# Moving the first pair of w_in ahead of x, and both even products of Q in front of its odd ones

## The chip, the cores and the metric

The kernel runs on one core of a Trainium2 chip. The metric is the device time of one execution in microseconds (us). The profile's span is 1.7 to 3.0 us shorter than the time of the same run, 1.8 in most. The granted clock is the share of TensorE's full clock that the profile records: 1.00 is full, 0.50 half. PE is TensorE, DVE is VectorE, ACT is ScalarE, POOL is GpSimd; SPq and ACTq are the queues from which the sync and the scalar engine issue transfers.

## The reference

```python
# x: (8, 3008, 256), float32; w_in: (256, 2048), w_out: (2048, 256), float64; result float32
X = np.fft.fft(np.fft.fft(x, axis=1), axis=2).real      # mixing
h = X.reshape(8 * 3008, 256) @ w_in
return (np.maximum(h, 0) ** 2 @ w_out)                  # squared ReLU between two products
```

## The kernel before

The transform over the sequence is done by products with cosine and sine tables (cosT, sinT) of folded x; that gives Pt, Qt and Et. The transform over the 256 columns is folded into w_in: G is w_in multiplied by small tables (cosd, sind, altd). The weights come as float64, and each pair of column blocks of w_in ("pair j", eight in all) is first rounded to float32, partly on VectorE, partly on ScalarE. `load_win(j)` issues the transfer and the first part of the rounding; what it returns finishes it and multiplies:

```python
def convert(dst, src):
    ...                                        # raw <- transfer of the pair's 64-bit words
    nc.vector.tensor_scalar(out=eb, in0=high, ...)              # fd<-raw
    act(e, eb, AF.Relu, ...); act(eb, e, AF.Relu, ...)          # fd<-fd, ScalarE
    nc.vector.tensor_scalar(out=mb, in0=high, ...)              # fs<-raw
    act(rest, low, AF.Copy, scale=2.0 ** -32)                   # raw<-raw, ScalarE
    def finish():
        nc.vector.scalar_tensor_tensor(out=eb, ...)             # fd<-raw,fd
        tt(out=m, in0=mb, in1=rest, op=ALU.add)                 # fs<-fs,raw
        nc.vector.scalar_tensor_tensor(out=dst, ...)            # win<-fs,fd
    return finish

def load_win(j):
    w = ep.tile(...)
    finish = convert(w, pair_in(j))
    def then():
        finish()
        for tab, G, n in ((cosd, G1, P), (sind, G2, P - 1)):
            ps = psh.tile([P, CH], F32, name="pg", tag="h")
            ... # pg: 2 products each, copied to G by ScalarE
        ps = psd.tile([P, CH], F32, name="pe", tag="d")
        ...     # pe: 4 products of one column, copied to gE
    return then
```

A transform (`group`) has an even product, two joins on VectorE, and an odd product; the even and odd results lie in tiles of PSUM (the memory that the products here are written to), named "pd", of a pool with two buffers (`psd`), which the pe tiles share. Then comes the main loop over the 8 batches; its first eight steps still round and multiply pairs 2 to 7 and the blocks of w_out.

The first phase of the kernel before, in order of issue (cut):

```python
for t in range(NT):                    # NT = 7 tiles of x
    load_x(0, t)
load_table(cosT, cos_s, nc.sync)
load_table(sinT, sin_s, nc.sync)
for dst, src in ((cosd, cos_d), (sind, sin_d), (altd, alt_d)):
    nc.sync.dma_start(out=dst, in_=...)
...                                    # fold x, make Pt and Et, fold for Q
begun = weights.pop(0)()               # pair 0: transfer, first part of rounding
for f in groups[16:20]:                # Q, rows of even number: even product, joins, odd product
    f()
next_weight()                          # begin pair 1; finish and multiply pair 0
for f in groups[20:]:                  # Q, the other half
    f()
next_weight()                          # begin pair 2; finish and multiply pair 1
```

## Time and profile before

| | before |
|---|---|
| median of the first three runs | 2075.13 us (2070.41 to 2075.86) |
| span of the profiled run | 2067.1 us |
| TensorE busy | 2004.5 us, 97% of the span |
| TensorE not busy | 62.6 us: 41.6 before 122 us, 10.5 in the last 51.7 us |
| median over all 35 timed runs of this study | between 2070.06 and 2072.77 us by set of runs (2067.44 to 2075.86) |

What is not TensorE's work is 62.6 us, 3% of the span, so what a new order of the first phase can take from TensorE's waiting is a few per cent at most. Time at half clock counts as busy here (from 62.24 to 71.80 us TensorE is busy for 9.55 of 9.56 us, at a granted clock of 0.54); the experiments come back to it. The views that carry this, windows and chain of waits, stand in the prediction.

### The profile page before, as it was taken

Reading aid. Unit: us, or ns where it says so; the run is one execution under the profiler, and the core shown is the slowest. Engines: PE = TensorE matmul, PEld = TensorE weight load, DVE = VectorE, ACT = ScalarE, POOL = GpSimd, SP = SyncE. Lnnn points to the kernel's source line nnn. Section 1 sums busy time; section 2 is a strip of 40 time slices with the busy share of each in tenths; the row PEclk is TensorE's granted clock in tenths of the full one; section 3 lists DMA queues with packets and bytes.
Section 4 is the critical chain, followed back from the end, with each engine's and each line's share of the span. In section 5 each row is a group of like instructions: output and inputs, shape, how many; then the busy total and the mean of one; then the engine's idle time right before and its main releaser. Section 6 shows DMA issues by size and latency. Waiting matters only on the chain.

```text
span 2067.1 us, 27083 instructions
## 1 busy us (share of the span) xinstructions
PE 2004.5 (97%) x9464; PEld 1742.9 (84%) x9464; DVE 1334.7 (65%) x3271; ACT 949.4 (46%) x1069; POOL 1202.6 (58%) x1766
## 2 busy tenths in 40 slices
PE   5799999999999999999999999999999999999997
PEld 3688888888888888888888888888888888888887
DVE  6798665776567755677557775577656775555553
ACT  1554444444444543455444544454444444445443
POOL 0376555665566654666556665566655675456565
PEclk9899999999999999999999999999999999999999
DMA  5333000110011010011001100011001100000000
GB/s 168 91 62 59 29 11 31 41 35 21 11 40 41 26 31 26 26 31 46 11 26 36 38 28 11 31 41 36 21 11 40 41 11 21 26 11 11 21 11 20
DMA packets 66104, 68.45 MB, mean 33 GB/s; under 512 B 26297, under 2 KB 56969, under 8 KB 65968
## 3 DMA queue, kind: packets, MB, share of 16 engines
q1 hardware_dynamic: 65968, 66.73, 11.4%
q8 instruction: 74, 1.21, 0.3%
q14 instruction: 62, 0.51, 0.1%
HBM read 42.03 MB, written 24.68 MB: 32 GB/s over the span
## 4 chain that ended last, share of the span: by engine, by line
PE 94%; DVE 3%; DMA 1%; ACT 0%; issue 0%; SPq 0%; POOL 0%; POOLq 0%; ACTq 0%; DVEq 0%
PE ph L410 16%; PE mA L450 16%; PE ph L411 16%; PE mC L450 16%; PE mB L450 15%; PE mD L450 8%; PE pd L350 5%; PE po L484 2%; PE pg L234 1%; DMA xt<-in_x_dram 1%; ACT os L486 0%; DVE he L413 0%; PE pe L240 0%; DVE g L416 0%; DVE g L415 0%
## 5 line engine op out<-in xcount | busy, mean ns | idle before, releaser
L424 ACT ACTIVATE g<-g 128x1004 f32<-128x1004 f32 (+1 forms) x384 | 399.4, 1040 | 828.0 <-DVE g L416 551.9
L413 DVE SCALAR_TENSOR_TENSOR he<-Et,gE,ph 128x251 f32<-128x251 f32 (+1 forms) x768 | 362.2, 472 | 591.9 <-PE ph L411 591.2
L430 POOL TENSOR_TENSOR s<-g 128x251 f32<-128x251 f32 (+1 forms) x384 | 251.7, 655 | 686.3 <-ACT g L425 662.6
L410 PE MATMUL ph<-Pt,G 128*128 128x251 f32 (+1 forms) x1536 | 452.4, 375 | 0.4 <-DVE g L416 0.3
L411 PE MATMUL ph<-Qt,G 127*128 127x251 f32 (+1 forms) x1536 | 451.2, 374 | 0.0
L425 ACT ACTIVATE g<-g 128x1004 f32<-128x1004 f32 (+1 forms) x384 | 399.2, 1040 | 12.2
L450 PE MATMUL mA<-g,wout 128*128 128x251 f32 (+1 forms) x1536 | 389.5, 375 | 0.0
L450 PE MATMUL mC<-s,wsum 128*128 128x251 f32 (+1 forms) x1536 | 389.4, 374 | 0.0
L415 DVE TENSOR_TENSOR g<-he,ph 128x251 f32<-128x251 f32 (+1 forms) x768 | 320.5, 417 | 58.9 <-DVE he L413 0.5
L410 PEld LDWEIGHTS ph<-Pt,G 128*128 128x128 f32 x1536 | 287.8, 189 | 41.9 <-issue 3.2
L411 PEld LDWEIGHTS ph<-Qt,G 127*128 127x128 f32 x1536 | 291.2, 190 | 35.8
L450 PEld LDWEIGHTS mC<-s,wsum 128*128 128x128 f32 x1536 | 291.6, 190 | 35.2
L450 PEld LDWEIGHTS mA<-g,wout 128*128 128x128 f32 x1536 | 284.9, 189 | 39.8 <-issue 4.0
L416 DVE TENSOR_TENSOR g<-he,ph 128x251 f32<-128x251 f32 (+1 forms) x768 | 314.2, 409 | 0.0
L431 POOL TENSOR_TENSOR s<-s,g 128x251 f32<-128x251 f32 (+1 forms) x384 | 287.0, 747 | 30.1
L432 POOL TENSOR_TENSOR s<-g 128x251 f32<-128x251 f32 (+1 forms) x384 | 290.4, 756 | 0.0
L433 POOL TENSOR_TENSOR s<-g,s 128x251 f32<-128x251 f32 (+1 forms) x384 | 263.0, 685 | 0.0
L450 PE MATMUL mB<-g,wsum 128*128 128x251 f32 (+1 forms) x768 | 225.1, 374 | 0.0
L450 PE MATMUL mD<-s,wout 128*128 128x251 f32 (+1 forms) x768 | 225.0, 374 | 0.0
L450 PE MATMUL mB<-s,wout 128*128 128x251 f32 (+1 forms) x768 | 224.6, 374 | 0.0
L450 PEld LDWEIGHTS mB<-g,wsum 128*128 128x128 f32 x768 | 145.6, 190 | 17.7
L450 PEld LDWEIGHTS mD<-s,wout 128*128 128x128 f32 x768 | 144.9, 189 | 18.1
(73 smaller groups left out, 1317.5 us busy)
## 6 DMA issues: line engine op xcount, KB each, us to landing
xt<-in_x_dram SPq DMA_DIRECT2D x24, 512.0 KB
out_dram<-os SPq DMA_DIRECT2D x96, 125.0 KB
out_dram<-os SPq DMA_DIRECT2D x80, 126.0 KB
xt<-in_x_dram SPq DMA_DIRECT2D x16, 384.0 KB
Et<-e_dram SPq DMA_DIRECT2D x7, 752.5 KB
raw<-in_moe_w_in_dram SPq DMA_DIRECT2D x16, 256.0 KB
raw<-in_moe_w_out_dram SPq DMA_DIRECT2D x16, 256.0 KB
xt<-in_x_dram SPq DMA_DIRECT2D x8, 480.0 KB
```

What stands on the lines that cost most here:

```text
L410: nc.tensor.matmul(hP, G1[:, fs], pt[:, ks], start=True, stop=True)
L411: nc.tensor.matmul(hQ, G2[:, fs], qt[:, ks], start=True, stop=True)
L413: nc.vector.scalar_tensor_tensor(out=t, in0=et[:, ks], scalar=gE[:, fc:fc + 1], in1=hP, op0=ALU.mult, op1=ALU.add)
L415: tt(out=g[:, h, 0, 0:n], in0=t, in1=hQ, op=ALU.add)
L416: tt(out=g[:, h, 1, 0:n][:, ::-1], in0=t, in1=hQ, op=ALU.subtract)
L424: act(v, v, AF.Relu)
L425: act(v, v, AF.Square)
L430: gt(out=s1, in0=g21, in1=g22, op=ALU.add)
L431: gt(out=s2, in0=s1, in1=g11, op=ALU.subtract)
L432: gt(out=s3, in0=g11, in1=g21, op=ALU.subtract)
L433: gt(out=s4, in0=g12, in1=s2, op=ALU.subtract)
L450: nc.tensor.matmul(acc[nm][:, i, 0:n], w, v[:, 0:n], start=j == 0 and i == 0, stop=j == NJ - 1, skip_group_check=True)
```

## The change

Its intent: the rounding of pair 0 is done while x is still arriving and VectorE has nothing to do (before the change it was idle for 5.68 us up to 19.57), and Q's two halves are no longer separated by a pair. The small tables, which pair 0 needs, are issued from the scalar engine.

```diff
-    for t in range(NT):
-        load_x(0, t)
...
-    load_table(cosT, cos_s, nc.sync)
     make_identity(nc, ident)
-    load_table(sinT, sin_s, nc.sync)
...
-        nc.sync.dma_start(out=dst, in_=src.rearrange("(c p) m -> p c m", p=P))
+        nc.scalar.dma_start(out=dst, in_=src.rearrange("(c p) m -> p c m", p=P))
...
+    begun = weights.pop(0)()
+    for t in range(NT):
+        load_x(0, t)
+    load_table(cosT, cos_s, nc.sync)
+    load_table(sinT, sin_s, nc.sync)
+    start()
+    for_p(0)
+    begun()
-    for t in range(4):
+    for t in range(1, 4):
         for_p(t)
...
     begun = weights.pop(0)()
-    for f in groups[16:20]:
-        f()
-    next_weight()
-    for f in groups[20:]:
-        f()
+    groups_at(16, 20, 17, 18, 19, 21, 22, 23)
     next_weight()
```

Groups 16 to 19 are the even product, the two joins and the odd product of Q's first half, 20 to 23 those of the second.

More of the change, by code (lines that the diff above doesn't have):

```diff
@@ L494, in ahead, with next_weight @@
         return ops + [(0.0, lambda: load_e(b))] if b else ops
+    weights = [lambda j=j: load_win(j) for j in range(2)]
+    for j in range(NJ):
+        if j + 2 < NJ:
+            weights.append(lambda j=j: load_win(j + 2))
+        weights.append(lambda j=j: load_wout(j))
+    def next_weight():
+        nonlocal begun
+        then, begun = begun, weights.pop(0)() if weights else None
+        then()
     pieces = [[f for _, f in fold(0, t)] for t in range(NT)]
-    begin, *groups = [f for _, f in dft_ops(0)]
-    begin()
+    start, *groups = [f for _, f in dft_ops(0)]
     def for_p(t):
@@ L524 @@
         groups_at(*((3, 7), (8,), (9, 10), (11, 12), (13, 14), (15,), ())[n])
-    weights = [lambda j=j: load_win(j) for j in range(2)]
-    for j in range(NJ):
-        if j + 2 < NJ:
-            weights.append(lambda j=j: load_win(j + 2))
-        weights.append(lambda j=j: load_wout(j))
-    begun = weights.pop(0)()
-    def next_weight():
-        nonlocal begun
-        then, begun = begun, weights.pop(0)() if weights else None
-        then()
-    for f in groups[16:20]:
-        f()
-    next_weight()
-    for f in groups[20:]:
-        f()
+    begun = weights.pop(0)()
+    groups_at(16, 20, 17, 18, 19, 21, 22, 23)
     next_weight()
```

## The prediction

> **What bounds the kernel now.** I read the share of busy time first, then the span in slices, then the windows of the first 130 us, and last the chain of waits with the timeline of the first 65 us, because the change touches nothing later.
>
> ```profile
> span 2067.1 us, 27083 instructions
> PE 2004.5 (97%) x9464; PEld 1742.9 (84%) x9464; DVE 1334.7 (65%) x3271; ACT 949.4 (46%) x1069; POOL 1202.6 (58%) x1766
> ...
> PE   5799999999999999999999999999999999999997
> ```
>
> TensorE is busy for 97% of the span. All that it does not use is 2067.1 - 2004.5 = 62.6 us, and the row of slices (51.7 us each) says where: in the first two, and a little in the last. Between the second and the last slice there is nothing to win by order alone. So the stage to look at is the head, in 10 us windows (columns: stretch, its length, busy time and instructions of PE, PEld, DVE, ACT, POOL, then the granted clock, the DMA share and GB/s):
>
> ```profile
> 10.00:20.00 10.00, 3.78 (x12) 2.74 (x13) 4.10 (x14) 0.24 (x1) 0.00 (x0) 1.00 0.72 187
> 20.00:30.00 10.00, 9.72 (x27) 5.37 (x27) 8.73 (x25) 0.25 (x2) 0.00 (x0) 1.00 0.76 197
> 30.00:40.00 10.00, 7.17 (x22) 4.00 (x22) 9.59 (x29) 0.47 (x2) 0.00 (x0) 0.84 0.81 234
> 40.00:50.00 10.00, 5.22 (x14) 2.58 (x13) 7.46 (x21) 3.65 (x7) 0.00 (x0) 0.81 0.00 0
> 50.00:60.00 10.00, 7.84 (x30) 5.60 (x30) 3.10 (x9) 1.66 (x6) 0.00 (x0) 0.83 0.18 54
> 60.00:70.00 10.00, 7.75 (x22) 6.59 (x23) 6.45 (x13) 5.03 (x10) 0.00 (x0) 0.54 0.34 105
> ```
>
> Up to 15 us nothing is multiplied; from 20 to 42 us VectorE is the fuller engine; from 42 to 62 us neither PE nor DVE is full, so they wait for one another. The chain that ended last, cut to this stage, names the waits in order of time:
>
> ```profile
> 3.51 11.18 DMA xt<-in_x_dram
> 14.69 0.02 issue
> 14.71 2.52 DMA cosT<-in_cos_s_dram
> 17.23 0.14 issue
> 17.36 1.91 PE pd L350 x4
> ...
> 42.77 4.27 PE pd L350 x8
> ...
> 50.72 3.58 PE pg L234 x8
> 54.29 0.79 PE pe L240 x8
> 55.08 3.49 PE pd L350 x14
> ...
> 62.24 3.78 PE pg L234 x8
> ```
>
> Read it in three parts. To 17.36 us the start hangs on the queue of transfers: x (3 MB), then the cosine table behind it. From there to 42.77 us it runs mostly through VectorE. Then come, one after another: Q's first half (42.77), pair 0 of w_in (50.72, releasing the product that makes G), Q's second half (55.08), pair 1 (62.24). The two pauses of PE in it, 3.70 and 3.69 us, both end on the rounded pair:
>
> ```profile
> 50.72 2.07 PE L234 MATMUL pg<-win,cosd 128*128 128x256 f32 x4 [3.70 <-DVE win L219]
> ...
> 62.24 2.08 PE L234 MATMUL pg<-win,cosd 128*128 128x256 f32 x4 [3.69 <-DVE win L219]
> ```
>
> [...] In the kernel before all goes through one queue[...]; it does show that the engines are full (256 to 341 GB/s in each stretch from 2 to 12 us, by 2 us windows). [...] the granted clock is 0.81 to 0.84 in the windows from 30 to 60 us and 0.54 from 60 to 70, and a product 128x377 takes 769 ns at its record there against 481 in the steady part. It follows that no size of a PE step in this stage is firm. [...] the copy da<-pd of Q's first half starts at 45.22 us, directly after the three activations of a pair (43.29, 44.04, 44.67).
>
> **The change, part by part.** Instruction counts don't change on any engine; only places do.
>
> *Part 1, transfers: it costs.* Ahead of x now go pair 0 (2 x 256 KB) and, on the other queue, cosd, sind, altd (128 + 127 + 1 KB): 768 KB, or 786 kB. At the rate of the stretch from 6 to 12 us (303, 341 and 271 GB/s in three 2 us windows, mean 305) that is 2.6 us. x, the cosine table and with them the first product of PE come later by that: 17.36 becomes about 20.0 us. The order of the remaining transfers is the same, and so is the limit of eight in flight that makes the later cosine pieces wait for x. This is on the path.
>
> *Part 2, pair 0 in the gap: it is free.* The pair lands at about 6 us. Its rounding on VectorE is two tensor_scalar (0.42 each), then 0.68 + 0.68 + 0.69: 2.9 us; the activations 0.72 + 0.72 + 0.66 = 2.1 us run beside the fold of x tile 0. VectorE before was idle from 13.88 us, when it had folded five tiles, to 19.57 us: 5.7 us. Folding five tiles takes 5 x 1.79 = 9.0 us from the landing of the first (4.87 + 2.6 = 7.5); with the 2.05 us of the pair's last part in between this ends at 18.5 us, against 22.2 us when it is next needed (19.57 + 2.6). So VectorE swallows it. PE does the pair's 16 instructions at about 11.5 to 16 us, when it had nothing to do.
>
> *Part 3, pair 0 leaves the stretch 42.77 to 62.24: it gains.* Off the path go there the tensor_scalars (0.66 by issue spacing), the last three (1.93) and PE's 3.58 + 0.79 = 4.37: 7.0 us in all.
>
> *Part 4, the even products together: mixed.* What takes the place is worked out from the same durations, in the clock of the trace before, starting at 42.77. The two tensor_scalars of pair 1 and its activations stay in front of the copy da: the joins of the first half again start at 45.47 and end at 46.55. Meanwhile PE does both even parts. Q's four products have only two PSUM buffers among them, and both even ones now hold one, so the first odd product cannot begin until the joins of the first half have released theirs: PE starts it at 46.6, where before it ran at once behind the even one. Six instructions of 376 columns: 1.9 us at full clock (the steady "x6 1.90" of the chain), 3.65 when all are cold (4.27 less two of 189 columns); I take 2.9: 49.5. Then Qt takes 1.0 (50.5); only then, by VectorE's order, come the joins of the second half, 1.07 (51.6), since its buffer too must be released; the second odd product, 2.6 (54.2); Qt 1.05 (55.3); two tensor_scalars of pair 2, 0.67 (55.9); the end of pair 1, 1.93 (57.9). PE can start on pair 1 at 57.95 instead of 62.24.
>
> The sum: -4.3 us there (7.0 removed, 2.7 given back by the odd products that now wait for joins), +2.6 us at the start: -1.7 us. [...] I take **-1.9 us**. From pair 1 on, order and durations are those of before, and the chain is VectorE rounding to 122 us, PE after it; so the gain should arrive at the end as it is.
>
> **Rivals.** *A, the transfers cost nothing* because the head is bound elsewhere: then the whole 4.3 us is gained, 2069.5. For it: DMA has a weak stretch (48 GB/s from 14 to 16 us) into which a little could be tucked. Against: that stretch comes from the eight-in-flight limit behind x and moves with x; and the chain waits on DMA without a break from 3.5 to 17.36. *B, the delay is paid in full and the merged even products gain little*, because both odd products run cold after PE's new pauses (about 1.3 and 2.1 us): 3.65 instead of 2.9 and 2.6 costs 1.8 us, the sum is then 0. Time 2074. For it: each half-clock stretch in this trace follows a pause of PE. Against: each of the new pauses is shorter than 3.7. *C, VectorE becomes the bound in the first 20 us*: if the small tables and the pair land late (past 9 us), fold and rounding end after 22 us and the delay grows, +2 us. Against: 3.7 us of slack in part 2. *D, all of it is off the path*, as PE catches up later: the 65% of VectorE and the full PE after 122 us speak against; PE has no idle time there in which to make good a later start.
>
> **Range and chances.** The three timed runs before span 2070.41 to 2075.86, median 2075.13; their mean is 2073.8, which I take as the level to subtract from. 2073.8 - 1.9 gives about **2072 us**. The mechanism is uncertain by about +-1.5 us (rivals A and B), the median of some runs by +-2 or 3 us[...]. Together 8 in 10: **2067.5 to 2076**. Two per cent would be 41.5 us; all idle PE time of the first 122 us is under 60, and the change touches two pauses of 3.7. Chances: faster 0.01, within 2% 0.98, slower 0.01.
>
> **What would show it right or wrong.** In the profile after: PE's first cosine products wait for DMA to about 18 us and the 128x189 ones start near 20.0 (17.36 now); pair 0's products stand at 11 to 16 us; VectorE has no wait longer than some tenths on the pair; PE starts pair 1 at 60 to 61 (57.95 + 2.6) with a pause of about 3.7 before it still, released by VectorE's win; two new pauses of PE in front of the odd products of Q, released by VectorE's dc; and the steady stage, PE without pause, begins some 2 us before 121 us. The prediction is wrong if the first product is not later (A), if pair 1 begins at 62 or after (B), or if the fold of x waits for the scalar engine or ends past 22 us (C).

## The result, and the profile after

| | before | after |
|---|---|---|
| median | 2072.77 us (2069.83 to 2075.86, 4 runs) | 2066.17 us (2063.89 to 2066.92, 4 runs) |
| span, profiled run | 2067.1 us | 2062.1 us |
| ratio | | 0.9966 (0.9946 to 0.9986) |

A ratio is the mean time of one kernel's fast runs over that of the other's of the same rounds, so it is not quite the ratio of the medians. The change gains 0.34%, about 7 us, where 1.9 were predicted; the median lies 1.3 us below the range.

The windows of the kernel after (cut), columns as in the prediction (after the busy times: granted clock, DMA share, GB/s):

```profile
10.00:20.00 10.00, 6.71 (x20) 5.48 (x20) 8.65 (x24) 0.91 (x3) 0.00 (x0) 1.00 0.77 205
...
60.00:70.00 10.00, 8.30 (x40) 6.95 (x39) 7.50 (x17) 5.46 (x13) 1.83 (x4) 0.87 0.48 156
```

The first line shows pair 0 in its new place: TensorE has 6.71 us of work between 10 and 20 us instead of 3.78, VectorE 8.65 instead of 4.10. The last shows something the prediction did not have: the granted clock between 60 and 70 us is 0.87, where it was 0.54. The chain of waits, first the start, then Q and pair 1:

```profile
17.30 2.62 DMA cosT<-in_cos_s_dram
19.92 0.14 issue
20.06 1.91 PE pd L345 x4
...
45.01 3.30 PE pd L345 x10
...
48.89 3.85 PE pd L345 x6
...
53.83 2.18 PE pd L345 x6
...
59.69 3.40 PE pg L229 x8
63.09 0.80 PE pe L235 x8
```

The start is later by 2.70 us (17.36 before); pair 1 begins at 59.69 where it began at 62.24. Between these two points the change gains back the transfers' price and 2.55 us more; the prediction's sum to this point was 1.7. That it took 1.9 was the author's estimate; the 16 cosine products from the start on take 7.41 us in both profiles, the 22 products behind them 6.96 before and 6.51 after. The rest comes behind it. These are TensorE's products for pairs 1 and 2, before:

```profile
64.11 1.91 PE L234 MATMUL pg<-win,sind 128*127 128x256 f32 x4
65.82 1.71 PE L240 MATMUL pe<-altd,win 128*128 128x1 f32 x8
67.39 2.05 PE L234 MATMUL pg<-win,cosd 128*128 128x256 f32 x4
69.23 1.91 PE L234 MATMUL pg<-win,sind 128*127 128x256 f32 x4
```

and after:

```profile
61.56 1.53 PE L229 MATMUL pg<-win,sind 128*127 128x256 f32 x4
62.93 0.95 PE L235 MATMUL pe<-altd,win 128*128 128x1 f32 x8
63.74 1.11 PE L229 MATMUL pg<-win,cosd 128*128 128x256 f32 x4
64.69 1.03 PE L229 MATMUL pg<-win,sind 128*127 128x256 f32 x4
```

The same products take 1.91 us (69.23) or 1.03 (64.69), and 2.05 (67.39) or 1.11 (63.74). From the start of pair 1 to the first product of the main loop (ph) it was 62.24 to 71.80, 9.56 us, and is 59.69 to 66.36, 6.67 us: 2.9 us gained by instructions that the change did not touch. The lead of 5.4 us (pair 3 begins at 78.00 before, at 72.56 after) then shrinks to 5.0 at the end of the span.

### The profile page after: what moved, and what is told of

It is laid out like the page before. It is cut to its first block, busy times and chain, and to the rows that moved or that the text cites. A ratio compares the mean times of both kernels' runs of the same rounds, so it can differ in the third digit from the quotient of the medians.

```text
span 2062.1 us, 27082 instructions
## 1 busy us (share of the span) xinstructions
PE 2004.4 (97%) x9464; PEld 1742.7 (85%) x9464; DVE 1335.1 (65%) x3271; ACT 949.4 (46%) x1069; POOL 1204.8 (58%) x1766
## 4 chain that ended last, share of the span: by engine, by line
PE 95%; DVE 3%; DMA 1%; ACT 1%; issue 0%; POOL 0%; POOLq 0%; SPq 0%; ACTq 0%; DVEq 0%
PE ph L405 16%; PE mA L445 16%; PE mC L445 16%; PE ph L406 16%; PE mB L445 16%; PE mD L445 8%; PE pd L345 5%; PE po L479 2%; PE pg L229 1%; DMA xt<-in_x_dram 1%; ACT os L481 0%; DVE he L408 0%; DVE fd L211 0%; DVE fs L213 0%; DVE g L411 0%
```

## The experiments

Theory 1: the unforeseen part comes from TensorE's clock. In the profile of before it is at half for 3.41 us from 50.55 and for 10.24 us from 60.79, where the two pauses of 3.70 and 3.69 us end (50.72 and 62.24); the change removes one of these pauses. Rivals: chance (2), and the merged order of Q itself (3). The runs came in three sets, each on a chip of its own beside its own runs of the kernel before; across sets the ratios to these are compared. The first four kernels below are the first set, beside 11 runs of the kernel before (2068.50 to 2075.04, median 2070.76).

**The changed kernel again.** No edit.

> The changed kernel once more, to separate chance from effect. Theory 1 (the part of the gain that was not foreseen, some 3 to 5 us, comes from TensorE's clock: pairs 1 and 2 are multiplied at full clock because fewer pauses precede them): again 4 to 8 us under before, ratio 0.996 to 0.998, and the granted clock of its runs on the average above that of before. Rival 2 (the four runs were lucky, the true gain is the predicted 1.9 us): ratio about 0.999. In the profile the first 128x189 products start at 20.0 +-0.4 either way.

Measured: 2066.13 us (2064.57 to 2068.33), ratio 0.9979 (0.9966 to 0.9992), first 128x189 products at 20.53. The gain is real: 4.7 us by the means, at the lower end of what theory 1 expected. The granted clock is little higher, 0.9904 on the average of the runs against 0.9891 before, which alone would prove nothing.

**Pair 0 early, Q in the old order.**

```diff
-    groups_at(16, 20, 17, 18, 19, 21, 22, 23)
+    groups_at(16, 17, 18, 19, 20, 21, 22, 23)
```

> The change without its last part: pair 0 ahead of x, but Q's products in the old order, odd one of the first half directly behind its even one. By the working of the prediction the merged order costs about 2.5 us, because an odd product waits for joins to free a PSUM buffer: pair 1 then starts near 57 us instead of 59.7 and the kernel takes 2 to 3 us less than the changed one (ratio 0.995). If the merged order is the source of the unforeseen gain (theory 3: two even products together keep the array busy and warm), this is slower than the changed kernel by 3 us or more (ratio 0.998).

Measured: 2063.18 us (2061.66 to 2067.07), ratio 0.9964 (0.9952 to 0.9976): 2.7 us less than the changed kernel of the same set by the means, though the two groups of five runs overlap and the changed kernel's first four runs had nearly the same ratio, 0.9966. Pair 1 starts at 57.32 instead of 59.69. It is not slower by 3 us, so theory 3 falls; that the last part of the change costs, as worked out, is settled only with the dummy products below.

**Only the merged order of Q**, on the kernel before.

```diff
-    for f in groups[16:20]:
-        f()
-    next_weight()
-    for f in groups[20:]:
-        f()
+    groups_at(16, 20, 17, 18, 19, 21, 22, 23)
+    next_weight()
     next_weight()
```

> The kernel before with only the order of Q changed: both even products together, then pair 0 and pair 1 one behind the other. By durations at fixed clock: pair 1 starts at about 62.3 as before, gain 0 +-1 us. Theory 1 (clock): pair 1 follows pair 0 on TensorE without a pause, so pairs 1 and 2 run warm, gain 2 to 4 us (ratio 0.998 to 0.999). Theory 3 (merged order is the source): gain 4 us or more.

Measured: 2067.64 us (2063.96 to 2070.12), ratio 0.9982 (0.9970 to 0.9995): 3.6 us gained, where durations at a fixed clock gave 0 +-1. In its trace pairs 0 and 1 follow one pause together, and pair 1 runs at full clock:

```profile
56.36 2.08 PE L234 MATMUL pg<-win,cosd 128*128 128x256 f32 x4 [3.69 <-DVE win L219]
...
60.42 1.11 PE L234 MATMUL pg<-win,cosd 128*128 128x256 f32 x4
```

One pause of 3.69 us stands in front of two pairs, where the kernel before has 3.70 in front of pair 0 and 3.69 in front of pair 1.

**Only the order of the transfers**: pair 0 and the three tables ahead of x, but pair 0 rounded and multiplied where it was.

```diff
+    def fetch(src):            # the transfer alone, split off from convert
+        ...
+    for dst, src in ((cosd, cos_d), ...): nc.scalar.dma_start(...)
+    early.append(fetch(pair_in(0)))
     for t in range(NT):
         load_x(0, t)
...
-        raw = pool.tile(...); nc.sync.dma_start(...)
+        raw = early.pop(0) if early else fetch(src)
```

> The kernel before with only the order of transfers of the changed one (pair 0 and the three tables ahead of x); pair 0 is rounded and multiplied where it was. All theories that hold the price of the transfers real: the first 128x189 products at 20.0, everything to 60 us later by 2.3 to 2.7 us, time 2 to 3 us more than before (ratio 1.001). Rival A of the prediction (transfers free): ratio 1.000 and 17.4 us.

Measured: 2078.23 us (2071.62 to 2079.63), ratio 1.0029 (1.0015 to 1.0043), first 128x189 products at 21.01. Transfers are not free. But the price is 6 us by the means, not 2 to 3. Its trace has the products of pair 0 and of Q's second half at half clock:

```profile
57.69 1.71 PE L241 MATMUL pe<-altd,win 128*128 128x1 f32 x8
59.26 6.80 PE L351 MATMUL pd<-sinT,wQ 95*127 95x94 f32 x14
```

The 14 products of Q's second half took 3.61 us in the profile of before. The fastest run of this kernel, at a granted clock of 0.991, took 2071.62, which is 2.8 us above the three runs of before with the same clock (about 2068.8). So about half of the 6 us is put down to the clock; no run of this kernel with dummies checks it.

The next step was to take the clock away as a variable: dummy products in TensorE's pauses. They write the tile of the pe products, which these then overwrite, so the result is unchanged. The number in front of each pair was chosen to fit its pause. The second set (the next two kernels, and the two with interleaved transfers further down) ran beside 11 other runs of the kernel before (2067.44 to 2075.57).

```diff
+    WARM = (6, 6, 0, 7, 7, 1, 2, 1)      # (0, 6, 0, 7, 7, 1, 2, 1) where pair 0 is early
         def then():
             finish()
+            pe = psd.tile([P, CH], F32, name="pe", tag="d")
+            for _ in range(WARM[j]):
+                nc.tensor.matmul(pe, ident, cosd.rearrange("p c m -> p (c m)"), start=True, stop=True)
...
-            ps = psd.tile([P, CH], F32, name="pe", tag="d")
+            ps = pe
```

**The kernel before with dummy products.**

> The kernel before with dummy products (cosd by the identity, into the tile of the pe products, overwritten by these) in the pauses in front of the pairs of w_in: 6 before pairs 0 and 1, 7 before pairs 3 and 4, 1 or 2 before 5 to 7. They add 30 products of 0.5 us at full clock to pauses in which TensorE waits anyway, so by durations at a fixed clock nothing can be gained. Theory 1 (clock): pairs 0, 1, 2, 3, 4, 6 run warm and the kernel gains 5 to 9 us (ratio 0.996 to 0.9975) and the granted clock rises above 0.993. If the clock is not on the path (theory 3): 0 to 2 us slower.

Measured: 2060.66 us (2060.14 to 2061.45), ratio 0.9946 (0.9932 to 0.9961): 10.9 us by the means, more than was expected, from adding work. The spread of the runs shrank from 8.1 us to 1.3. The windows show the clock at full:

```profile
50.00:60.00 10.00, 8.89 (x43) 6.76 (x42) 4.65 (x12) 3.21 (x8) 0.00 (x0) 1.00 0.16 52
60.00:70.00 10.00, 8.86 (x49) 7.99 (x49) 8.69 (x18) 6.30 (x14) 1.84 (x4) 1.00 0.49 157
```

and the timeline shows the dummies in the pause, and the pair after it in half the time (2.08 us before):

```profile
57.27 2.75 PE L235 MATMUL pe<-cosd,ident 128*128 128x256 f32 x12
61.12 1.13 PE L239 MATMUL pg<-win,cosd 128*128 128x256 f32 x4 [1.10 <-DVE win L219]
```

**The changed kernel with dummy products.**

> The changed kernel with the same dummy products in the pauses in front of pairs 1 and 3 to 7. Theory 1: 3 to 6 us under the changed kernel (ratio to before 0.9945 to 0.996), and only 0 to 3 us under the kernel before with dummies, because with the clock held up in both what is left of the change is the 1 to 2 us worked out from durations. Theory 3 (the rest of the gain is of the order itself): still 5 us or more under the kernel before with dummies.

Measured: 2060.71 us (2060.39 to 2060.93), ratio 0.9946 (0.9932 to 0.9960). Against its ratios without dummies, 0.9966 and 0.9979, that is 4 to 7 us gained (0.0020 and 0.0033 of 2071), and there is no difference left to the kernel before with dummies. In the spans of the runs, 2058.4 against 2058.9 on the average, the change keeps half a microsecond. So with the clock held up the change as a whole is worth nothing that these runs resolve.

**Control: the early tile, no dummy product.** `WARM = (0, 0, 0, 0, 0, 0, 0, 0)` on the kernel before. This, the next two and the last experiment ran in a third set beside 9 runs of the kernel before (2068.92 to 2075.47).

> Control for the dummy products: the kernel before with the tile of the pe products taken earlier, as there, but without one dummy product. Theory 1 (the products hold the clock up): as the kernel before, ratio 0.999 to 1.001, runs spread over 2067 to 2076. If the earlier tile was what gained: ratio near 0.9946.

Measured: 2069.67 us (2068.55 to 2075.80), ratio 0.9996 (0.9981 to 1.0012). It is the products, not the tile.

**Pair 0 early with Q in the old order, with dummies.**

> Pair 0 ahead of x, Q in the old order, dummy products in the pauses. With the clock held up only durations count: by the sums of the prediction the early pair gains 4.0 (7.0 less the warm products' 1.6, and Q's old order kept) less 2.6 for the transfers and some warm products, so 2 to 4 us under the kernel before with dummies, ratio to before 0.993 to 0.9945, and 2 to 4 us under the changed kernel with dummies, which has the merged order on top.

Measured: 2057.22 us (2055.90 to 2057.97), ratio 0.9930 (0.9917 to 0.9942): 3.3 us under both kernels with dummies by the ratios, as expected. (The sum in the expectation is wrong: 7.0 less 1.6 is 5.4, not 4.0; less 2.6 that gives 2.8.)

**Only the merged order, with dummies** (6 in front of pair 0, none in front of pair 1, 2 in front of pair 2).

> The kernel before with the merged order of Q alone, dummy products in the pauses (6 before pair 0, 2 before pair 2). With the clock held up the merged order saves a second wait for VectorE's rounding but adds the wait of the odd products for joins: 0 +-1.5 us against the kernel before with dummies, ratio to before 0.994 to 0.9955. If it is 3 us or more slower, the merged order costs the same without the early pair.

Measured: 2061.43 us (2061.29 to 2062.10), ratio 0.9952 (0.9939 to 0.9964). With the clock held up the merged order alone gains nothing, and loses 1 us if anything.

The two parts of the change, with and without the clock as a variable, each as the ratio to the kernel before of its own set (with dummies, the first and the last row are of the second set, the two between of the third):

| | as it is | dummies in the pauses |
|---|---|---|
| before | 1 | 0.9946 |
| merged order only | 0.9982 | 0.9952 |
| pair 0 early only | 0.9964 | 0.9930 |
| both (the change) | 0.9966, 0.9979 | 0.9946 |

**Transfers interleaved**: pair 0 early, Q in the old order, six small pieces of the cosine table issued between the tiles of x. In the profile of before the first eight transfers (the last of them at 4.00 us) are issued without a wait for a landing; then seven issues of pieces of the cosine table wait for a tile of x to land, 7.4 us in all.

```diff
+    table = load_table(cosT, cos_s, nc.sync)      # now a list of issues
     for t in range(NT):
         load_x(0, t)
+        if t:
+            table.pop(0)()
```

> Pair 0 ahead of x with Q's products in the old order, and six small pieces of the cosine table issued between the tiles of x, so that the limit of eight transfers in flight no longer leaves the queue empty behind x. If the stretch of weak transfer behind x is on the path: the first 128x189 products at 18.0 +-0.4 instead of 20.1, and 1 to 2 us under the version without this (ratio 0.9955). If VectorE's fold takes its place: no gain.

Measured: 2061.66 us (2060.11 to 2063.24), ratio 0.9951 (0.9937 to 0.9966). By the ratios it is some 2.7 us below the version without it, but from another set; the products in front of the 128x189 ones, of the class of 94 rows, waited to 18.99 for the last small piece of the table, issued behind the last tile of x, and the 128x189 ones followed at 19.68, so the 18.0 of the expectation was missed. Pair 1 starts at 56.57 instead of 57.32.

**All together**: the last one with dummies.

> All that helped so far together: pair 0 early, Q in the old order, cosine pieces between the tiles of x, dummy products in front of pairs 1 and 3 to 7. If the parts add: 4 to 6 us under the same without dummies, ratio to before 0.992 to 0.9945, the fastest of all.

Measured: 2056.21 us (2055.44 to 2058.39), ratio 0.9926 (0.9912 to 0.9941). It beats both kernels, by 15 us the one before and by about 10 the changed one (means of different sets), and is correct like all kernels here. Against pair 0 early with dummies (0.9930) the interleaving is worth under 1 us, which two sets of runs do not resolve.

**Eleven more dummies**, 4 behind pair 0 and 7 in the short pauses before the products of Et and Q.

> The fastest version so far with 11 more dummy products: 4 behind pair 0, 3, 1 and 3 in the short pauses in front of the products of Et and Q. If the half clock from 19 to 29, 39 to 42 and 46 to 49 us is on the path: another 1 to 3 us, ratio to before 0.991 to 0.9922. If VectorE alone sets the time there, no gain.

Measured: 2057.94 us (2055.83 to 2059.09), ratio 0.9931 (0.9918 to 0.9945). No gain. The 4 in front of the first cosine products ran from 16.57 us for 3.52 and pushed these back, to 19.93 us, so they were longer than the pause; and the clock was still at half from 26.5 to 33.4 and from 47.0 to 50.4 in its trace. Whether the others are worth nothing because VectorE sets the time there, the run does not show.

## Why the prediction was wrong

*What bounded the kernel* was misread in one place: "from 20 to 42 us VectorE is the fuller engine" holds only from 30 us on, since the window from 20 to 30 us has TensorE busy for 9.72 us and VectorE for 8.73. And of the 62.6 us 13.8 lie between the second and the last slice.

*Transfers, part 1: right.* 2.6 us were predicted; the first 128x189 products moved from 17.36 to 20.06 in the first pair of profiles. Over five profiles with the old order (16.70 to 17.93, mean 17.28) and six with the new (20.06 to 21.01, mean 20.43) it is 3.1. That the three tables count in full, though they are issued from the scalar engine, was the author's assumption; from 2 to 12 us the DMA engines moved 291 GB/s in the profile before, through one queue, and 279 in the one after, through two. No run issues the three tables from the sync engine, so that the second queue bought nothing is not shown by itself.

*Pair 0 in the gap, part 2: right.* The fold of five tiles ended at 19.1 us (18.5 predicted), and VectorE was next needed at 22.26 (22.2). TensorE did the pair from 12.01 to 17.3.

*Q, part 4: right in direction; right in size partly by luck.* From the last tile of wQ to pair 1 the sum gave 15.2 us (42.77 to 57.95); measured 14.7 (45.01 to 59.69). Two errors cancel: the first odd product took 3.85 us at half clock (0.50 from 48.92 to 52.33) instead of 2.9, and the second did not wait for the joins of its half (1.07 in the sum) but began at 53.83, as soon as Qt was done, and took 2.18 instead of 2.6. That the merged order gives back about 2.7 us was confirmed by undoing it: 2.7 us without dummies (runs overlapping), 3.3 with (0.9946 less 0.9930, of 2071). A better change was thus in sight in the prediction's own sum and was not named there: leave the order of Q alone.

*The step that failed* is this sentence of the prediction: "From pair 1 on, order and durations are those of before, and the chain is VectorE rounding to 122 us, PE after it; so the gain should arrive at the end as it is." The order was that of before, the durations were not. In the profile of before, pairs 1 and 2 were multiplied at half clock nearly throughout (9.56 us), after at half only for the first part of pair 1 (6.67): 2.9 us, more than the whole of the predicted gain. Part 3 has the same fault: it counts pair 0's products as 4.37 us, but at full clock they take 2.64 (51.17 to 53.81 in the kernel before with dummies). The prediction had seen the clock of 0.54 in that window, and then used the row's durations as if they belonged to the instructions. It allowed the runs +-2 or 3 us of either sign around the same mean, when the change, which leaves one of two pauses of 3.7 us, moves the mean.

That the clock is the cause, and not the order, is shown by the dummies: work added to the pauses, and nothing else, makes the kernel before 10.9 us faster and the changed one 4 to 7, and the difference between them disappears. The prediction's own terms then give it too: 7.0 less 1.7 for the warm products of pair 0, less 2.7 and 2.6, is 0. What the clock costs in the pauses before the pairs is thus 10.9 us in the kernel before and, by the ratios of the table, 4 to 7 in the three variants, all of which have one long pause fewer there. That the clock tells them apart, the dummies show; that the number of pauses does is argued from the traces. Behind the long pauses up to pair 1, TensorE is at half clock for 3.41 us in all five profiles that have one such pause and no dummies, and for 13.7 (twice) and 20.5 in the three that have two. The merged order alone has the clock and no other gain: 3.6 us faster as it is, no faster with the clock held up.

*The spread of before goes with the clock*, and the dummies take it away (1.3 us instead of 8.1). In the second set seven of the 11 runs lay at 2067.44 to 2070.61 with a granted clock of 0.990 or 0.991, and four at 2074.34 to 2075.57 with 0.986 to 0.988. Part of the predicted range's error is the level: 2073.8, from three runs of which two were of the slow group.

*Rivals.* A (transfers free) is refuted by the run with the transfers alone. B (the delay paid and both odd products cold, sum 0) came half true: the first odd product ran at half clock, the second took 2.18 us, and pair 1 began before 62. Its sum, 0, is also what the change is worth with the clock held up, but for another reason, the warm products of pair 0. C and D did not happen.

What stays open: which stretch of a given run falls to half clock. The records give the clock in pieces of 3.41 us and multiples of it, with edges that differ from run to run. The pause of 3.7 us in front of pair 1 is in both kernels, yet the half clock behind it lasts 10.24 us in the two profiles with the order of before (before and the control) and 3.41 in the four with pair 0 early and no dummies. In the two pair 1 starts 1.45 and 1.60 us behind an edge, in the four 0.11 to 0.53; no run separates this from the number of pauses. Why the kernel before falls into two groups in the second set, and into a spread in the first, was not pursued.

## What to carry to other kernels

Where TensorE waits now and then (half clock followed pauses of 1.8 to 4.3 us here), a duration read from a row holds only for the clock it ran at (four products of a pair took 1.91 or 1.03 us): before pricing a change, look at the granted clock of its window, and ask which pauses it adds and removes, since an unchanged instruction behind a removed pause may take half the time. To tell an order's worth from the clock's, fill the pauses with dummy products in both kernels and compare those; here the filled version was the better kernel too, by 10.9 us for the one before. And when a sum of parts shows one part giving back what another gains, run the parts alone: here half of the change was better than the whole (0.9930 against 0.9946 with dummies).

## What the records of the clock show

- A stretch that is full by busy time is not always followed by full clock. In the profile of before (columns: stretch, length, busy time of PE, PEld, DVE, ACT, POOL, granted clock, DMA share, GB/s) the second of these windows is 3.42 of 3.42 us busy, and the clock of the third is still half:

```profile
60.79:64.20 3.41, 1.96 (x5) 1.60 (x6) 3.33 (x7) 1.21 (x2) 0.00 (x0) 0.50 0.47 147
64.20:67.62 3.42, 3.42 (x14) 3.06 (x13) 1.45 (x3) 0.80 (x3) 0.00 (x0) 0.50 0.52 161
67.62:71.03 3.41, 3.41 (x10) 2.69 (x10) 1.87 (x3) 2.26 (x5) 0.00 (x0) 0.50 0.00 0
```

  The durations agree with the record: 1.91 us at 69.23 for products that take 1.03 at full clock. In the profile of the transfers alone the piece from 60.30 to 63.71 is full of Q's products, and the half clock lasts to 73.95; in the profile after, a piece busy for 2.88 of 3.41 us (59.16 to 62.57) is followed by full clock. So busy time, as the profile has it, does not decide alone; no run here shows what does.
- Pauses of 3.70 and 3.69 us are followed by half clock in the profile of before; with dummies, which leave 1.11 and 1.10 us of them, the clock of that kernel is 1.00 from 50 to 70 us. Shorter pauses stand in front of half clock too: in the kernel before with dummies the clock is at half from 37.00 to 40.41 and from 43.83 to 47.24 us, behind pauses of 1.95 and 0.89 and of 1.79 us. Filling pauses with products whose results are not used was worth 10.9 us of 2071.6 here, with the spread of the runs down from 8.1 us to 1.3.
- Those 10.9 us are 0.5% of the time of the kernel before, but several times the predicted effect of the change (1.9 us), and they decided whether it gained anything.
- The profile of before has its first record of the clock at 26.65 us; for the time in front of it the windows give 1.00, yet the 16 cosine products from 17.36 us take 7.41 us, to the hundredth what they take in the repeated run of the changed kernel from 20.53 us, where the record says 0.50.
